# A long convolution beside a mixer MLP: the transform's split turned from 32 by 64 to 64 by 32 tokens, its second stages in eight-frequency fp32 units, the token matrices in fp16 parts

## The chip, the core and the metric

The kernel runs on one core of one Trainium2 chip. The metric is device time in microseconds (us). The core's engines run side by side, and each takes its own instructions strictly in order: TensorE (PE in the profile) multiplies matrices into PSUM, VectorE (DVE) and ScalarE (ACT) work elementwise, SyncE (SP) and, for some transfers, ScalarE issue DMAs. PEld is TensorE's weight loading.

## The reference

The reference normalises the input's rows, convolves them along the 2048 tokens with a kernel built from 128 complex states per channel (512 channels), and multiplies by the gate of an MLP on the same normalised rows:

```python
xn = layernorm(x)                                      # 2048 x 512
P  = exp(dt*A [:, :, None] * l)                        # 512 x 128 x 2048, complex
K  = einsum("dn,dnl,dn->dl", C, P, dt*B).real
y  = irfft(rfft(pad(xn.T)) * rfft(pad(K)))[:2048].T + xn*Dskip
h  = gelu(layernorm(xn) @ w1)
hs = concat(shift(h0,+1), shift(h1,-1), shift(h2,+2), shift(h3,-2)) @ w2
x1 = xn + hs
g  = silu(x1 + gelu(layernorm(x1) @ w3) @ w4)           # w3: 512 x 1376
out = x + y*g
```

Shifts are along the tokens, each of a quarter of the channels.

## The kernel before, in words

**Token layout.** 2048 tokens are 16 blocks of 128 partitions. Token number is a row r or t times a stride plus a column, and the kernel's transform of length 4096 uses the same split: 32 rows (`L1`) by 64 columns (`L2`). The transform is evaluated at 32 shifted frequencies g of the rows times 64 frequencies m of the columns, and the zero padding costs no work. It has a first stage (sums over rows, for each g) and a second stage (sums over columns, one small matrix per g, because the twiddle factors sit in it); the way back has the same two in reverse order.

**Stages of the transform.** `u_stage1` multiplies two token blocks of the normalised rows X by the matrix `ks1`; the result `ue` goes to a DRAM scratch, `scr_Ud`. `tables(hf)` builds the convolution kernel in chunks of 32 channels, 8 chunks for each half hf of the channels: exponentials and sines on ScalarE (`mag`, `wv`), products on VectorE, 64 matmul pairs per chunk (`pc<-wv`), an evacuation `kev`, and, at the end of `sums`, the first stage of the kernel's transform, named ks below: four matmuls `pc<-kev,ks`, two copies into `k1e`, two DMAs into scratch `scr_Kfa` or `scr_Kfb` (a and b are the halves). `products(hf)` is the second stage: it loads constants `cst`, the first-stage results of the rows, `uin`, and of the kernel, `kin`; multiplies both by the second-stage matrices (kspec and uspec); multiplies the two spectra on VectorE (`kh` is the evacuated kernel spectrum, `pr` the products); multiplies back (inv, `pd<-pr,cst`), copies to `z1e`, and stores to scratch `scr_Zda` or `scr_Zdb`. `inverse(hf,g)` loads `zin` from there, multiplies by `is2`, and multiplies the result into X, which by then holds the gate; `finish` adds the residual `xr` and stores the output.

In `products`, half 0 works in fp32 on two frequencies at a time, 16 units. Half 1 has 8 units of four frequencies, in two steps of two; there the loaded `kin` and `uin` are split in fp16 high and low parts (`kx`, `uh`) with power-of-two scales that `spectrum_scale` takes from the kernel's size, and kspec and uspec are three fp16 passes each.

**The MLP.** `token_mixing` makes X, the first stage of the rows, `h_pair` (rows times w1, gelu, kept as fp32 `hT`), the token shifts (`wrapped`), and `hs_pair` (four fp32 matmuls per token block with w2, added to X). Of the eight pairs of blocks four take fp32 w1 with transposes on TensorE and four take fp16 parts with DMA transposes. `mlp(g)`, eight times, is the wide MLP in fp16 high and low parts with w3 and w4, in three passes.

**What sets the order.** The functions above do not issue instructions. They record operations, and each operation's dependencies are found from the 32-partition quarters of SBUF places and PSUM banks that it touches. The table `ORDER` at the head lists the operations' numbers in the order of issue (a suffix a or v puts an evacuation or a scaling that either engine can do on ScalarE or VectorE). So one recorded list is cut up and interleaved by hand-held numbers; all recorded instructions carry one line of the profile, L330, that of the helper that issues them. PSUM is eight banks: pairs a and b for the MLP, pairs c and d for table sums, ks, spectra and the inverse stages. `Ring(place, bytes, n)` is a set of n buffers used in turn.

## Time and profile before

| | |
|---|---|
| three runs | 535.1, 536.88 (median), 538.08 us |
| profiled execution, span | 536.6 us, 13619 instructions |
| TensorE busy | 516.5 us |
| VectorE busy | 489.8 us |
| ScalarE busy | 425.2 us |
| last ks stage on TensorE starts | 398.92 us |
| last MLP matmul ends | 518.7 us |
| granted TensorE clock until 520 us, and after it | 1.00, 0.81 |

A span runs from the first to the last instruction of one profiled execution; here the span and the median of the runs agree within 0.3 us. Busy times are shares of the whole span, and the kernel has stretches of different kinds: loads and parameters (0 to 20 us); first half of the tables with token mixing (20 to 236); second half of the tables with the MLP and half 0 of the products (236 to 400); half 1 of the products with the rest of the MLP (400 to 520); and the end. In the rows of instruction groups a form like `pd<-kin,cst 128*64 128x256 f32` is destination, sources, the tile of TensorE's array (rows times columns), the shape and type of the operand. An fp32 matmul stands as two records in the trace, an fp16 one as one.

### The profile page before, as it was taken

The page shows a single profiled execution, that of the slowest core. Times are in us where ns is not written, and L with a number is a line of the kernel's source. Part 1 is how long each engine was busy: PE and PEld are TensorE (multiplying, and loading weights), DVE is VectorE, ACT ScalarE, POOL GpSimd, SP SyncE. Part 2 cuts the span into 40 slices and gives each one's busy share as a digit, 9 for nine tenths or more (in the row PEclk, how much of TensorE's full clock was granted, in tenths as well). Part 3 has the DMA queues.
Part 4 walks back from the last instruction along what each step waited for, and adds up shares of the span by engine and source line. Part 5 has one row for each costly group of instructions (what it writes and reads, how often), then busy time and mean ns, then how long its engine had stood idle before and what let it go on. Part 6 is the DMA issues. An engine that isn't in the chain of part 4 may idle for free.

```text
span 536.6 us, 13619 instructions
## 1 busy us (share of the span) xinstructions
PE 516.5 (96%) x5628; PEld 332.4 (62%) x5628; DVE 489.8 (91%) x755; ACT 425.2 (79%) x692; POOL 0.7 (0%) x6
## 2 busy tenths in 40 slices
PE   8999999999999999999999999999899899999992
PEld 7787664554475766565765666575565667666631
DVE  4999999999999999999999999999877799997277
ACT  3999999899899999999799897868646566774340
POOL 0000000000000000000000000000000000000000
PEclk9999999999999999999999999999999999999997
DMA  8989975689677325356375738838889969896997
GB/s 228 214 268 257 230 200 155 190 132 127 158 188 118 46 36 60 42 68 112 120 137 148 150 108 167 145 94 176 149 170 169 348 201 297 261 280 226 314 277 205
DMA packets 212830, 93.50 MB, mean 174 GB/s; under 512 B 163297, under 2 KB 196065, under 8 KB 212385
## 3 DMA queue, kind: packets, MB, share of 16 engines
q1 hardware_dynamic: 208032, 88.18, 71.3%
q10 hardware_dynamic: 4736, 4.46, 2.8%
q8 instruction: 44, 0.72, 0.6%
q14 instruction: 18, 0.14, 0.1%
HBM read 56.96 MB, written 29.36 MB: 161 GB/s over the span
## 4 chain that ended last, share of the span: by engine, by line
PE 63%; DVE 12%; ACT 11%; DMA 7%; issue 3%; SPq 1%; DVEq 0%; ACTq 0%
PE pb L330 24%; PE pa L330 17%; PE pd L330 11%; PE pc L330 11%; DVE wv L330 4%; DMA scr_Kfb<-k1e 3%; DVE X L330 3%; ACT wv L330 2%; ACT mag L330 2%; ACT L330 2%; SPq L330 1%; DMA kin<-scr_Kfb 1%; DMA scr_Kfa<-k1e 1%; DMA cst<-c_gq 1%; ACT g L330 1%
## 5 line engine op out<-in xcount | busy, mean ns | idle before, releaser
L330 PE MATMUL pb<-x1T,w3h 128*128 128x256 f16 (+1 forms) x1056 | 125.1, 273 | 1.2 <-ACT g L330 1.2
L330 PE MATMUL pa<-w4h,ghl 128*128 128x512 f16 (+1 forms) x528 | 123.2, 380 | 0.0
L330 PEld LDWEIGHTS <-w3h 128*128 128x128 f16 (+1 forms) x1056 | 102.3, 100 | 27.8 <-issue 11.0
L330 PEld LDWEIGHTS <-ghl 128*128 128x128 f16 (+1 forms) x528 | 49.3, 98 | 59.1 <-issue 8.7
L330 ACT ACT_TABLE_LOAD x52 | 66.7, 1283 | 2.0 <-PEq L1347 1.2
L330 ACT ACTIVATE wv<-wv 128x2080 f32<-128x2080 int32 x32 | 63.0, 1968 | 0.3 <-DVE wv L330 0.3
L330 ACT ACTIVATE g<-pb,wsc 128x512 f32<-128x512 f32 (+1 forms) x48 | 30.6, 651 | 12.8 <-PE pb L330 11.5
L330 ACT ACTIVATE ghl<-g,wsc 128x512 f16<-128x512 f32 (+1 forms) x39 | 26.6, 688 | 13.3 <-PE pa L330 8.3
L330 DVE TENSOR_TENSOR wv<-wv,eg 128x2048 f32<-128x2048 f32 x16 | 36.5, 2284 | 0.1
L330 DVE TENSOR_TENSOR wv<-mag,wv 128x2048 f32<-128x2048 f32 x16 | 36.6, 2285 | 0.0
L330 PE MATMUL pd<-pr,cst 64*128 64x256 f32 x256 | 36.3, 402 | 0.0
L330 PEld LDWEIGHTS pc<-wv 128*32 128x32 f32 x2048 | 29.8, 109 | 9.7 <-issue 6.2
L330 PE MATMUL pc<-wv 128*32 128x64 f32 x2048 | 32.5, 220 | 2.7 <-issue 1.9
L330 DVE SCALAR_TENSOR_TENSOR ghl<-g,wsc,ghl 128x512 f16<-128x512 f32 (+1 forms) x48 | 33.5, 701 | 1.0 <-ACT ghl L330 0.8
L330 ACT ACTIVATE wv<-wv,halfpi 128x2080 f32<-128x2080 f32 x16 | 32.9, 2056 | 0.1
L330 ACT ACTIVATE mag<-par 128x128 f32<-128x128 f32 x132 | 32.8, 441 | 0.0
L330 ACT ACTIVATE kh<-pc,ksc 128x256 f32<-128x256 f32 (+1 forms) x40 | 20.1, 553 | 14.1 <-PE pc L330 12.5
L330 PEld LDWEIGHTS pd<-pr,cst 64*128 64x128 f32 x256 | 22.0, 186 | 11.5 <-issue 8.3
L330 PE MATMUL pb<-xT,w 128*128 128x256 f32 x128 | 29.0, 382 | 0.0
L330 PEld LDWEIGHTS pb<-xT,w 128*128 128x128 f32 x128 | 23.8, 190 | 5.5 <-issue 1.6
L330 PE MATMUL pb<-w,hT 128*128 128x512 f32 x58 | 26.9, 599 | 0.0
L330 DVE BATCH_NORM_STATS2 stats<-X 128x6 f32<-128x512 f32 x32 | 21.4, 681 | 5.3 <-DMA X<-in_A_u_dram 5.3
(167 smaller groups left out, 882.7 us busy)
## 6 DMA issues: line engine op xcount, KB each, us to landing
wst<-in_B_w_dram SPq DMA_DIRECT2D x20, 512.0 KB, 4.0
scr_Ud<-ue SPq DMA_DIRECT2D x32, 256.0 KB, 3.2
scr_Kfa<-k1e SPq DMA_DIRECT2D x16, 256.0 KB, 6.2
uin<-scr_Ud SPq DMA_DIRECT2D x16, 256.0 KB, 4.1
cst<-c_gp SPq DMA_DIRECT2D x16, 256.0 KB, 3.5
kin<-scr_Kfa SPq DMA_DIRECT2D x16, 256.0 KB, 3.6
scr_Zda<-z1e SPq DMA_DIRECT2D x16, 256.0 KB, 3.0
scr_Kfb<-k1e SPq DMA_DIRECT2D x16, 256.0 KB, 6.0
```

The lines of the kernel that those rows point to most:

```text
L330: ins = [getattr(self.engines[op.eng], name)(*args, **kw).ins for name, args, kw in op.calls]
```

## The change

The split is turned: 64 rows (`NA`) by 32 columns (`NI`), with 64 frequencies g of the rows and 32 of the columns. With it:

- X is loaded and stored in two pieces of 64 partitions rather than four of 32, and the token shifts' wrap runs over 64.
- `u_stage1` has four matmuls with 64 rows and 128 columns of the array, rather than eight of 32 by 64.
- ks has eight matmuls of 32 by 128, 256 wide, into all four banks of c and d, rather than four 512 wide into c; four copies rather than two; one DMA in pieces of 128 bytes rather than two in pieces of 64.
- `products` has 8 units in each half, each of eight frequencies, all fp32: 16 matmuls each for kspec, uspec and inv on tiles of 64 by 32 or 32 by 64. The fp16 splits of half 1, their scales, the squares that fed them and `spectrum_scale` are gone. Loads and stores of half 0 double to 512 KB. In half 0 there is one buffer each for `kin` and `uin` (two before), and `z1e` lies in the place of `uin`.
- `inverse` has four matmuls of 128 rows and 64 columns, rather than eight of 64 by 32.
- The token matrices go to fp16 parts: seven of eight pairs in `h_pair` (four before), `hT` as high and low parts, w2 as `w2h` with a scale of its own (`second_weights`), twelve fp16 matmuls per block in `hs_pair` rather than four fp32 ones.
- Chunks 8 to 15 of the tables and units 0 to 7 of half 0 are recorded in turn, and `ORDER` is a new table.

The counts in the two orders: DMAs on SP 296 before and 230 now, on ScalarE's queue 36 and 19; VectorE instructions 757 and 776, ScalarE's 708 and 698.

```diff
@@ the order, the first line of each table
 ORDER = """
-23 20 21 0 22 39 7 8 1 6 5 105 86 3 2 106 107 108 109 110 111 112 87 89 88 90 113 91 114 115a 92 93 94 95 25 24
+4 78 3 31 5 6 0 7 79 80 81 8 88 89 82 83 90 91 92 84 85 22 86 93 94 2 95 87a 96a 21 97a 103 105 104 106 107 108 109
...
@@ tables: the kernel's first stage
-        if cc >= 8:
-            A.activation(kg.rearrange("p d i -> p i d"), kev, AF.Square, accum_out=ssk[:, cc - 8 : cc - 7])
-        pk = bank[2]
-            for r in range(4):
-                T.matmul(pk[n][64 * c : 64 * c + 64], ks1[rows], kev[rows]..., start=True, stop=True)
-        for n in range(2):
-            E.copy(k1e[:, :, n], pk[n].rearrange("p (i d) -> p i d", d=8))
-        for c in range(2):
-            Q.dma_start(K1d[cc // 8][:, :, :, ch : ch + 16]..., k1e[64 * c : 64 * c + 64]...)
+        pk = bank[2] + bank[3]
+            for hi in range(2):
+                for r in range(4):
+                    T.matmul(pk[r][:, :DH], kk1[rows, hi], kev[rows, NI * hi : NI * hi + NI]...,
+                        start=hi == 0, stop=hi == 1)
+        for r in range(4):
+            E.copy(k1e[:, :, 8 * r : 8 * r + 8], pk[r][:, :DH].rearrange("p (i d) -> p i d", d=8))
+        Q.dma_start(K1d[cc // 8][:, :, :, ch : ch + CQ].rearrange("i e g d -> (e g) i d"), k1e)
@@ buffers of the products: half 0, then half 1
-            kin=Ring(early, K2, 2), uin=Ring(early + 2 * K2, K2, 2), cst=Ring(early + 4 * K2, K2, 2),
-            kh=Ring(early + 6 * K2, K2, 1), pr=Ring(early + 7 * K2, K2, 2), z1e=Ring(early + 9 * K2, K2, 1),
+            kin=Ring(early, K4, 1), uin=Ring(early + K4, K4, 1), z1e=Ring(early + K4, K4, 1),
+            cst=Ring(early + 2 * K4, K2, 2), kh=Ring(early + 3 * K4, K2, 2), pr=Ring(early + 4 * K4, K2, 2),
-            pr=Ring(o, K4, 4), kh=Ring(o + 4 * K4, K4, 2), z1e=Ring(o + 6 * K4, K4, 3),
-            kx=Ring(o + 9 * K4, K4, 2), uh=Ring(o + 11 * K4, K4, 2),
+            pr=Ring(o, K2, 8), kh=Ring(o + 4 * K4, K2, 4), z1e=Ring(o + 6 * K4, K4, 3),
@@ products(hf, steps), one unit of eight frequencies
+            def spectrum(pair, src):
+                    for ri in range(2):
+                        for c in range(4):
+                            for h in range(2):
+                                T.matmul(both[h][32 * c : 32 * c + 32, ri], fwd[rows, c, 32 * ri : 32 * ri + 32],
+                                    src[rows, c], start=True, stop=True)
+            kp = spectrum(bank[3 - hf], kin)
+            kh = [ring["kh"]([P, 2, DH], F32, "kh") for _ in range(2)]
+            for h in range(2):
+                E.copy(kh[h], kp[h])
+            up = spectrum(bank[3], uin)
+            for h in range(2):
+                t = ring["pr"]([P, 2, DH], F32, "pr")
+                V.tensor_mul(t, up[h], kh[h])
+                V.tensor_mul(kh[h][:, ::-1], up[h], kh[h][:, ::-1])
+                V.tensor_sub(t[:, 0], t[:, 0], t[:, 1])
+                V.tensor_add(t[:, 1], kh[h][:, 0], kh[h][:, 1])
+            pz = [t[:, :DH] for t in bank[2] + bank[3]]
+                for ri in range(2):
+                    for c in range(4):
+                        for h in range(2):
+                            T.matmul(pz[c][64 * h : 64 * h + 64], inv[rows, h, ri], z[h][rows, ri],
+                                start=ri == 0, stop=ri == 1)
+            for c in range(4):
+                E.copy(z1e[:, c], pz[c])
+            Q.dma_start(by_g(Zd[hf], un), z1e.rearrange("p g d -> p (g d)"))
@@ inverse, u_stage1
-            for r in range(4):
-                for a in range(2):
-                    T.matmul(py[a][32 * r : 32 * r + 32], is2[h], zin[h, r], start=True, stop=True)
+            for a in range(2):
+                for r in range(2):
+                    T.matmul(py[a][64 * r : 64 * r + 64], is2, zin[:, 2 * a + r], start=True, stop=True)
-                for r in range(4):
-                    T.matmul(pu[r][64 * a : 64 * a + 64], ks1[rows], X[rows, s + a], start=True, stop=True)
+                for r in range(2):
+                    T.matmul(pu[2 * a + r], ks1[rows], X[rows, s + a], start=True, stop=True)
@@ h_pair, hs_pair
-            A.activation(hv, ph, AF.Gelu_apprx_tanh, scale=1.0 if j < HF else a1)
+            A.activation(h32, ph, AF.Gelu_apprx_tanh, scale=1.0 if j < HF else a1)
+            E.affine(hv[0], h32, sh)
+            V.scalar_tensor_tensor(hv[1], h32, sh, hv[0], op0=ALU.mult, op1=ALU.subtract)
-                    T.matmul(acc[i], w, w2s[m], start=m == 0, stop=m == 3)
+                    for n, (lh, lw) in enumerate(PASSES):
+                        T.matmul(acc[i], w[:, lh], w2h[m // 2][:, m % 2, lw],
+                            start=m == 0 and n == 0, stop=m == 3 and n == 2)
-            V.tensor_add(X[:, s], X[:, s], acc[i])
+            V.scalar_tensor_tensor(X[:, s], acc[i], a2, X[:, s], op0=ALU.mult, op1=ALU.add)
...
```

**SP around the last kernel writes.** SP issues nearly all DMAs, and an issue waits on SP until what it needs is there. `scr_Zda<-z1e` is the store of a unit of half 0, `uin<-scr_Ud` the load of a later unit's rows, `scr_Kfb<-k1e` the write of a chunk of the kernel's first stage. Before:

```order
L330 DMA uin<-scr_Ud 128x512
L330 DMA kin<-scr_Kfa 128x512
L330 DMA_TRANSPOSE x1T<-x1h 128x8x128
L330 DMA cst<-c_gp 128x512
L330 DMA scr_Kfb<-k1e 64x64x16
L330 DMA scr_Zda<-z1e 128x512
L330 DMA scr_Kfb<-k1e 64x64x16
L330 DMA uin<-scr_Ud 128x1024 x2
L330 DMA_TRANSPOSE x1T<-x1h 128x8x128
L330 DMA scr_Zda<-z1e 128x512
L330 DMA scr_Kfb<-k1e 64x64x16 x2
```

Now:

```order
L314 DMA scr_Zda<-z1e 2x64x1024
L314 DMA uin<-scr_Ud 128x1x1024
L314 DMA scr_Kfb<-k1e 128x32x32
L314 DMA cst<-c_gp 128x512
L314 DMA kin<-scr_Kfa 128x1x1024
L314 DMA scr_Zda<-z1e 2x64x1024
L314 DMA uin<-scr_Ud 128x1x1024
L314 DMA kin<-scr_Kfa 128x1x1024
L314 DMA scr_Kfb<-k1e 128x32x32
L314 DMA scr_Zda<-z1e 2x64x1024
L314 DMA uin<-scr_Ud 128x1x1024 x2
L314 DMA scr_Kfb<-k1e 128x32x32
```

A unit's store and the next unit's row load now stand next to each other, since they share a place, and the kernel writes of the last chunks stand behind such a pair.

**PE around the last ks stage.** The rows with `kev` are the ks stage of chunk 15, `pa<-w4h,ghl` is the MLP, `kin` and `uin` begin a unit of half 0. Before:

```order
L330 MATMUL pd_98<-pr,cst 128x256
L330 MATMUL pd_99<-pr,cst 128x256
L330 MATMUL pc_96<-kev,ks_80 64x512
L330 MATMUL pc_97<-kev,ks_80 64x512
L330 MATMUL pc_96<-kev,ks_80 64x512
L330 MATMUL pc_97<-kev,ks_80 64x512
L330 MATMUL pd_98<-kin,cst 64x256 x4
L330 MATMUL pd_99<-uin,cst 64x256 x4
L330 LDWEIGHTS ghl
L330 MATMUL pa_92<-w4h,ghl 128x512
```

Now:

```order
L314 MATMUL pd_97<-pr,cst 64x256 x2
L314 MATMUL pd_98<-pr,cst 64x256 x2
L314 MATMUL pc_95<-wv 32x64 x64
L314 MATMUL pc_95<-kev,kk_90 128x256
L314 MATMUL pc_96<-kev,kk_90 128x256
L314 MATMUL pd_97<-kev,kk_90 128x256
L314 MATMUL pd_98<-kev,kk_90 128x256
L314 MATMUL pc_95<-kev,kk_90 128x256
L314 MATMUL pc_96<-kev,kk_90 128x256
L314 MATMUL pd_97<-kev,kk_90 128x256
L314 MATMUL pd_98<-kev,kk_90 128x256
L314 LDWEIGHTS ghl
```

The ks stage takes all four banks; the inverse of a unit of half 0 stands ahead of the chunk's sums, and MLP matmuls now follow at once, with the last unit's spectra behind them.

**VectorE, one unit of half 1.** `kx` and `uh` are the fp16 parts, `pr` the products, `z1e` evacuations of the inverse. Before, most of one unit:

```order
L330 TENSOR_SCALAR kh<-pc_96,ksc 128x256
L330 TENSOR_TENSOR pr<-pc_97,kh 128x1024
L330 TENSOR_TENSOR pr<-pr 128x2x256
L330 COPY z1e<-pd_98 128x256
L330 TENSOR_SCALAR kx<-kin,ksc 128x1024
L330 SCALAR_TENSOR_TENSOR kx<-kin,ksc,kx 128x1024
L330 TENSOR_TENSOR pr<-pc_97,kh 128x1024
L330 SCALAR_TENSOR_TENSOR uh<-uin,uh 128x1024
L330 TENSOR_TENSOR pr<-pr 128x2x256
```

Now, a whole unit:

```order
L314 TENSOR_TENSOR pr<-pd_97,kh 128x512
L314 TENSOR_TENSOR pr<-pd_98,kh 128x512
L314 TENSOR_TENSOR kh<-pd_97,kh 128x2x256
L314 TENSOR_TENSOR kh<-pd_98,kh 128x2x256
L314 TENSOR_TENSOR pr<-pr 128x256
L314 TENSOR_TENSOR pr<-kh 128x256
L314 TENSOR_TENSOR pr<-pr 128x256
L314 TENSOR_TENSOR pr<-kh 128x256
L314 COPY z1e<-pc_96 128x256
```

The splits are gone, and all eight products and sums of a unit now stand in one row between its uspec and its inverse stage.

461 lines of the change are left out of this document (200 added, 261 removed), and 7 rows, old and new, of the table ORDER.

## The prediction

> **What bounds the kernel now.** I read the busy shares, then the stretches, then the chain of waits at the change from the tables to half 1, then single rows.
>
> ```profile
> PE 516.5 (96%) x5628; PEld 332.4 (62%) x5628; DVE 489.8 (91%) x755; ACT 425.2 (79%) x692; POOL 0.7 (0%) x6
> PE 63%; DVE 12%; ACT 11%; DMA 7%; issue 3%; SPq 1%; DVEq 0%; ACTq 0%
> ```
>
> By these two lines TensorE bounds it: 96% busy and 63% of the chain that ended last. The stretches say more (columns: stretch, length, busy time and count of PE, PEld, DVE, ACT, POOL, granted clock, DMA share, GB/s):
>
> ```profile
> 0.00:20.00 20.00, 17.09 (x117) 16.00 (x118) 12.25 (x46) 10.61 (x19) 0.70 (x6) 1.00 0.95 236
> 20.00:236.00 216.00, 213.59 (x2198) 134.76 (x2198) 212.02 (x335) 207.86 (x353) 0.00 (x0) 1.00 0.69 146
> 236.00:400.00 164.00, 160.91 (x2080) 102.96 (x2082) 159.06 (x203) 134.52 (x209) 0.00 (x0) 1.00 0.65 133
> 400.00:520.00 120.00, 118.38 (x1113) 76.52 (x1113) 94.32 (x149) 71.55 (x113) 0.00 (x0) 1.00 0.94 267
> 520.00:536.57 16.57, 6.56 (x128) 2.13 (x128) 12.10 (x25) 0.65 (x1) 0.00 (x0) 0.81 0.73 209
> ```
>
> Up to 400 us VectorE works 12.25 + 212.02 + 159.06 = 383.3 us and is idle for 16.7; TensorE is idle for 8.4. Both are full, so taking work from TensorE alone wins little there. Behind 400 TensorE is full and VectorE idle for 26 of 120 us. The last rows are an end of 16.6 us that VectorE fills. The boundary near 400 us is the last ks stage, and what follows it is a wait (start, us, what):
>
> ```profile
> 402.93 9.37 DMA scr_Kfb<-k1e
> 412.35 5.86 DMA kin<-scr_Kfb
> ```
>
> ```profile
> 398.92 1.09 PE L330 MATMUL pc<-kev,ks 32*64 32x512 f32 x8
> 487.23 1.13 PE L330 MATMUL pd<-pr,cst 64*128 64x256 f32 x8
> 518.68 0.66 PE L330 MATMUL pd<-zin,is 64*32 64x256 f32 x16
> ```
>
> So the span has four pieces: 400 to the last ks; 18.3 until kin of half 1 has landed (412.35 + 5.86); 70 of half-1 units until the last inverse stage ends (488.3); 48.3 behind it, of which 17.9 follow the last MLP matmul at 518.7. I forecast each piece. The profiled span is 536.6 us and the runs' median 536.9, so the sum needs no correction.
>
> **Ahead of the last ks: VectorE.**
>
> ```profile
> L330 DVE SCALAR_TENSOR_TENSOR ghl<-g,wsc,ghl 128x512 f16<-128x512 f32 x40 | 29.7, 745 | 0.9 <-ACT ghl L330 0.8
> L330 DVE COPY ue<-pa 128x512 f32<-128x512 f32 x6 | 4.0, 685 | 0.0
> ```
>
> Added: 16 splits of hT at the 0.745 us of the same form for ghl, 11.9; 14 splits of x2 at 0.745 in place of 8 subtractions of that width, at the 0.690 of the widest sum of pr in a later fence, +4.9; two splits of w2 at the 1.28 of the row of kx there and a chain of short operations for its scale, together about +4; 16 updates of X at 0.745 in place of additions from PSUM, at the 0.685 of the products there, +1. Gone: nine copies of ue, which the new order gives to ScalarE, -6.2; scalings and copies that the same order moves or drops, about -3.6. Sum +12: 395 us of VectorE work ahead of the last ks. ScalarE gains some 19 there (353 to 372) and TensorE loses 19 although 22 us of MLP have been moved ahead. With one engine clearly fullest its idle time should not grow beyond the 16.7 of now, nor vanish, since 7.8 of it lie in the first 20 us: 10 to 17. I take 15, last ks at **410**, 10 later than before.
>
> **TensorE** is relieved everywhere:
>
> ```profile
> 267.51 1.13 PE L330 MATMUL pd<-pr,cst 64*128 64x256 f32 x8
> 268.57 1.09 PE L330 MATMUL pc<-kev,ks 32*64 32x512 f32 x8
> 22.47 0.65 PE L330 MATMUL pa<-X,ks 32*64 32x512 f32 x2
> 23.52 1.99 PE L330 MATMUL pb<-xT,w 128*128 128x256 f32 x8
> 269.59 1.08 PE L330 MATMUL pd<-kin,cst 128*64 128x256 f32 x8
> 270.50 1.03 PE L330 MATMUL pd<-uin,cst 128*64 128x256 f32 x8
> 428.40 0.82 PE L330 MATMUL pc<-uh,cst 128*64 128x256 f16 x12
> 429.16 1.47 PE L330 MATMUL pa<-w4h,ghl 128*128 128x512 f16 x6
> 430.55 1.13 PE L330 MATMUL pd<-pr,cst 64*128 64x256 f32 x8
> 519.14 0.64 PE L330 MATMUL pc<-zin,is 64*32 64x256 f32 x16
> 85.37 10.46 PE L330 MATMUL pa<-w,hT 128*128 128x512 f32 x24
> L330 PE MATMUL pb<-x1T,w3h 128*128 128x256 f16 x960 | 113.7, 273 | 1.2 <-ACT g L330 1.2
> ```
>
> I go from start to start. Half 0 paid 0.91 twice and 1.06, 2.9 us in each of 16 steps, 46. A new stage is 16 small fp32 matmuls; the nearest row is the 64 by 32 tiles of zin, eight matmuls from 518.68 to 519.14, 0.46, so 0.92, and I take 0.95: 24 stages, 23 (-23). Half 1 paid 0.76 for each three-pass spectrum and 1.06 for the inverse, 2.58 in 16 steps, 41, and now pays 23 too (-18). w2: 64 fp32 matmuls at 10.46/12 = 0.87 were 56; 192 fp16 ones at 1.39/6 = 0.232 are 45 (-11). Three more pairs with fp16 w1, about -5. Against it, `u_stage1` pays two rounds of 0.87 rather than the 1.05 of 22.47 to 23.52, 8 times, +6; `inverse` two rounds of 0.46 for one, 16 times, +7; ks 8 matmuls, four side by side, two rounds of 0.46, nothing. Together about -45. None of it shortens the first piece, since VectorE is the fuller engine there; its worth shows only behind the last ks.
>
> **The wait for the kernel's spectrum.**
>
> ```profile
> scr_Kfb<-k1e SPq DMA_DIRECT2D x16, 256.0 KB, 6.0
> scr_Zdb<-z1e SPq DMA_DIRECT2D x8, 512.0 KB, 5.8
> uin<-scr_Ud SPq DMA_DIRECT2D x8, 512.0 KB, 5.7
> kin<-scr_Kfb SPq DMA_DIRECT2D x8, 512.0 KB, 6.0
> zin<-scr_Zdb SPq DMA_DIRECT2D x8, 512.0 KB, 7.0
> ```
>
> In the new order the last kernel write stands on SP behind the row load of half 0's last unit, which waits for the store of the unit before. That unit's inverse ends some 2 us ahead of the last ks (64 table matmuls stand between), so its 512 KB store, at the 5.8 us of half 1, lands about 4 behind it, and the write is issued there rather than after the 1 us that its four copies take. Write 6.0, load 6.0: 4 + 12 = **16**, against 18.3 now, where the write took 9.4. Pieces twice as long could make the write faster (3.0 us is what half 0's store of 256 KB in rows takes); a crowded stretch makes it 9.4. Bounds 13 to 20.
>
> **Eight units of half 1.** The constants row is a small load and hidden. Before, a step spread over the MLP; now each unit is in TensorE's order the same: kspec, uspec, 4.2 us of MLP (six w4 matmuls, 1.39, and two runs of twelve w3 matmuls at 113.7/960 = 0.118), inverse. VectorE stands between:
>
> ```profile
> L330 DVE TENSOR_TENSOR pr<-pd,kh 128x512 f32<-128x512 f32 x32 | 21.4, 685 | 0.6 <-ACT kh L330 0.2
> L330 DVE TENSOR_TENSOR pr<-pr 128x256 f32<-128x256 f32 x32 | 13.0, 422 | 0.4
> L330 DVE TENSOR_TENSOR pr<-pc,kh 128x1024 f32<-128x1024 f32 x16 | 19.5, 1222 | 1.7 <-ACT kh L330 1.3
> L330 DVE TENSOR_TENSOR pr<-pr 128x512 f32<-128x512 f32 x16 | 11.0, 690 | 0.4
> L330 DVE SCALAR_TENSOR_TENSOR kx<-kin,ksc,kx 128x1024 f16<-128x1024 f32 x8 | 10.3, 1282 | 0.2
> L330 DVE SCALAR_TENSOR_TENSOR uh<-uin,uh 128x1024 f16<-128x1024 f32 x8 | 9.7, 1216 | 0.0
> L330 ACT COPY z1e<-pd 128x256 f32<-128x256 f32 x47 | 16.2, 375 | 11.9 <-PE pd L330 10.2 <-DMA xr<-in_A_u_dram 1.5
> ```
>
> VectorE's half 1 falls from 19.5 + 11.0 + 10.3 + 9.7 = 50.5 us to 64 operations, 35.4. But four products at 0.685 and four sums at 0.422, 4.4 us, now stand in one chain between a unit's uspec and its inverse, with the 4.2 us of MLP beside them and hand-offs and a split of ghl among them: TensorE waits 0.4 to 1.1. The inverse writes all four banks of c and d, so the next kspec waits for two copies of bank c (0.375, one on each engine, with hand-offs 0.6). A unit is 3 x 0.95 + 4.2 + 0.6 + 0.4 to 1.1 = 8.0 to 8.8; I take 8.3, so **66**, against 70 now. All MLP without waits would be 7.05; without cover by the MLP a unit is 3 x 0.95 + 4.4 + 1.2 = 8.5.
>
> **The end.** Behind the last inverse the new order has 11.2 us of MLP (42 w4 matmuls at 0.232, 12 w3 at 0.118) and 28 zin matmuls, two at a time, 6.4: 17.6. Then follow, as now, products and residuals on VectorE and the last store, 17.9 in the trace; half of the zin work has the longer `inverse`, but VectorE sets the pace there (TensorE has 6.56 of 16.57 us). That is **35**, against 48.3. A second path agrees: the store of the last unit 1 + 5.8 and its reload 7.0 put the first reload at 14, and 13 reloads of 512 KB with three smaller loads, some 7 MB, take 26 at the 267 GB/s of the fourth stretch; the last inverse, product, sum and store add about 6, so 32. Range 31 to 40.
>
> Sum: 410 + 16 + 66 + 35 = **527**, which is +10, -2, -4 and -13 on the 536.6.
>
> The Trainium skill, "TensorE: Matmul & The Clock Gate", Part 3, "Measured speedup vs the span model", speaks against the small tiles: it gives four row tiles 3.07 times and sixteen tiles 10.6 times the rate of one matmul, which I read as an estimate of some 5.6 times for eight. By it a stage would take 16 x 0.46 / 5.6 = 1.3 us, and 24 stages behind the last ks 8 us more. The zin rows show eight tiles in the time of one, and go against it.
>
> **The rivals.**
>
> *The single place of uin and z1e in half 0 (slower).* A unit's row load waits until the unit before it has been stored, so one turn is uspec 0.95, chain 4.4 and hand-offs 1, inverse 0.95, copies 1, two issues 0.8, store, load: 9.1 plus 5.8 + 5.7 by half 1's rows of 512 KB, 20.6; by half 0's own rows,
>
> ```profile
> scr_Zda<-z1e SPq DMA_DIRECT2D x16, 256.0 KB, 3.0
> uin<-scr_Ud SPq DMA_DIRECT2D x16, 256.0 KB, 4.1
> ```
>
> 16.2, were size free. Half 0 runs at a DMA share of 0.65, not 0.94, so I place it near 17 to 18. By VectorE's work between successive uspecs in the new order, turns have 25.6, 17.1, 31.7, 19.1, 16.1, 15.2 and 11.7 us. At 17 the last three lag by 8, of which 5 fit in the idle time I allowed; at 20.6 the lag is 16 to 20, the last ks comes near 425, and the time is **542**. It decides from a turn of about 20.
>
> *The units serialise, and the end follows.* If hand-offs, ScalarE's copies of kh and the ghl splits make a unit 9.3 us, and SP's queue of half-1 loads and stores (0.94 DMA share now) holds the end at 37, it is 410 + 16 + 74.5 + 37 = **537**, no change. For it: nothing covers more than 4.2 us. Against it: VectorE has only about 7 us of work in a unit.
>
> *The tiles run less side by side.* From the trace, if they keep only the rate of the 32 by 64 tiles of `u_stage1` (8 x 0.87 in 1.05, 6.6 times), a stage takes 1.1 and the time is **531**; with 1.3, 535.
>
> *Better.* The order closes VectorE's idle time to 8, the write takes 4, units run at 7.5: 403 + 13 + 60 + 34 = **510**.
>
> **How the numbers follow.** Chances: likeliest 0.47 (own range 518 to 534), single place 0.17, serialised units 0.15, tiles 0.06, better 0.15. This kernel's measurement can tell 0.5%, 534.2 to 539.6, from no change. Faster: 0.45 + 0.15 + 0.04 and a little of the two middle rivals, 0.68; same 0.14, mostly from serialised units; slower 0.18. The range goes from the better case to the single place: 511 to 542.
>
> **What would show it.** Last ks at 407 to 414 with VectorE idle for 10 to 17 ahead of it. If it is later and the wait before uspec names the load of uin, the first rival is right. First half-1 kspec 13 to 20 behind it; stages of 0.9 to 1.0; units 8.0 to 8.8 apart; last MLP matmul 17 to 19 behind the last inverse. I am wrong in the main if VectorE ahead of the last ks falls short of 390 us or if units are over 9.

## The result

| | median of the runs, us | lowest to highest | ratio to before, 95% interval |
|---|---|---|---|
| before | 537.48 (4 runs) | 535.1 to 540.35 | |
| after | 915.66 (4 runs) | 913.75 to 918.92 | 1.703 [1.695, 1.710] |

The change makes the kernel 70% slower. The forecast was 527 with a range to 542, and none of the rivals reaches the measured time. Below, "after" is the changed kernel and "before" the one it came from.

The page of after, first the busy times, then the two lines of the chain that ended last:

```profile
PE 521.1 (57%) x6292; PEld 325.1 (36%) x6292; DVE 478.4 (52%) x774; ACT 414.8 (45%) x693; POOL 0.7 (0%) x6
DMA 46%; ACT 14%; DVE 13%; PE 11%; SPq 10%; issue 5%; ACTq 0%; DVEq 0%
DMA uin<-scr_Ud 14%; DMA scr_Zda<-z1e 10%; SPq L314 10%; DMA scr_Zdb<-z1e 6%; DVE wv L314 6%; ACT wv L314 3%; PE pd L314 3%; PE pa L314 3%; PE pb L314 3%; ACT mag L314 3%; DMA zin<-scr_Zda 2%; DMA scr_Kfb<-k1e 2%; DMA kin<-scr_Kfb 2%; PE pc L314 2%; DMA kin<-scr_Kfa 2%
```

Before, TensorE was 96% busy and 63% of the chain. Now no engine is busy for more than 57% of the span, and 46% of the chain are transfers, the units' loads and stores first. The stretches show where (stretch, length, busy time and count of PE, PEld, DVE, ACT, POOL, granted clock, DMA share, GB/s; cut at 250 us, at the last ks stage, at the first kspec of half 1, and at the end of the last inverse stage):

```profile
0.00:250.00 250.00, 224.12 (x2307) 149.66 (x2311) 231.24 (x397) 228.14 (x401) 0.70 (x6) 0.97 0.63 149
250.00:571.60 321.60, 177.58 (x2692) 111.70 (x2680) 163.43 (x211) 143.23 (x227) 0.00 (x0) 0.78 0.32 61
571.60:629.00 57.40, 12.29 (x136) 5.28 (x137) 10.25 (x22) 8.10 (x14) 0.00 (x0) 0.61 0.22 65
629.00:848.50 219.50, 74.90 (x990) 42.35 (x990) 48.28 (x98) 25.50 (x40) 0.00 (x0) 0.65 0.31 78
848.50:911.90 63.40, 32.21 (x182) 16.09 (x182) 25.17 (x48) 9.88 (x12) 0.00 (x0) 0.76 0.70 212
```

Up to 250 us VectorE is busy for 231 us, 92% of the time, and TensorE for 90%. From there to 848.5 us every engine is idle for much of the time, and the DMA queues are too: a share of 0.22 to 0.32 at 61 to 78 GB/s, where half 1 of before had 0.94 at 267 GB/s. So the transfers are late, and yet the engines that carry them are two thirds idle. The waits (engine, line, what for: us in all, times, longest):

```profile
PE pd L314 <- DMA uin<-scr_Ud: 159.5, 8, 39.2
DVE pr L314 <- PE pd L314: 204.8, 15, 40.5
```

Two turns of half 0 in the chain (start, us, what):

```profile
316.23 12.84 DMA scr_Zda<-z1e
329.09 13.08 DMA uin<-scr_Ud
355.87 13.43 DMA scr_Zda<-z1e
369.32 12.78 DMA uin<-scr_Ud
```

A turn takes 355.87 - 316.23 = 39.6 us, of which store and load are 25.9; the first rival had 20.6 for it, with 5.8 + 5.7 for the two transfers. Within the store from 356 to 369 us:

```profile
356.00:369.00 13.00, 7.66 (x97) 5.60 (x96) 9.16 (x12) 10.91 (x31) 0.00 (x0) 0.89 0.12 42
```

A share of 0.12 of 16 DMA engines is about two engines. The packet records of the trace say the same. Counted from them: how many packets of 4096 bytes there were in a stretch, how long one took, and how many were under way at once, most often (while any was) and at most:

```
kernel   stretch, us      packets   median ns   at once: most often   at most
after    356 to 369           128         159                      2         4
before   412.3 to 413.6        95         159                     16        19
```

A packet takes the same 159 ns as before, but two are under way most of the time (77% of it) and not sixteen. 512 KB are 128 packets, 64 for each of two engines: 64 x 0.159 = 10.2 us; the chain has 12.8 to 13.4 from issue to landing.

What the transfers have in common is their form in the order. In half 1 of before, `scr_Zdb` and `uin` were `128x1024`, and kin of the same shape. In the changed kernel the scratch side of a unit is `r s e (h g) d -> h (r s e) (g d)` with h = 2: 64 rows of 4 KB for each half of the frequencies, and the order prints the store as `2x64x1024`. The outermost count of that side is 2. This holds for uin, kin and z1e of all 16 units, 48 transfers.

### The profile page after: what moved, and what is told of

Read it like the earlier page. It is cut to its first block, busy times and chain, and to the rows that moved or that the text cites. A ratio compares the mean times of both kernels' runs of the same rounds, so it can differ in the third digit from the quotient of the medians.

```text
span 911.9 us, 14810 instructions
## 1 busy us (share of the span) xinstructions
PE 521.1 (57%) x6292; PEld 325.1 (36%) x6292; DVE 478.4 (52%) x774; ACT 414.8 (45%) x693; POOL 0.7 (0%) x6
## 4 chain that ended last, share of the span: by engine, by line
DMA 46%; ACT 14%; DVE 13%; PE 11%; SPq 10%; issue 5%; ACTq 0%; DVEq 0%
DMA uin<-scr_Ud 14%; DMA scr_Zda<-z1e 10%; SPq L314 10%; DMA scr_Zdb<-z1e 6%; DVE wv L314 6%; ACT wv L314 3%; PE pd L314 3%; PE pa L314 3%; PE pb L314 3%; ACT mag L314 3%; DMA zin<-scr_Zda 2%; DMA scr_Kfb<-k1e 2%; DMA kin<-scr_Kfb 2%; PE pc L314 2%; DMA kin<-scr_Kfa 2%
## 5 line engine op out<-in xcount | busy, mean ns | idle before, releaser
L314 PE MATMUL pb<-x1T,w3h 128*128 128x256 f16 (+1 forms) x1056 | 136.7, 290 | 23.1 <-DMA x1T<-x1h 19.2
L314 PEld LDWEIGHTS <-w3h 128*128 128x128 f16 (+1 forms) x1056 | 108.7, 106 | 56.8 <-issue 24.0
L314 DVE TENSOR_TENSOR pr<-pd,kh 128x512 f32<-128x512 f32 x32 | 20.8, 686 | 204.8 <-PE pd L314 204.8
L314 PE MATMUL pd<-uin,cst 64*32 64x256 f32 x512 | 29.4, 591 | 159.5 <-DMA uin<-scr_Ud 159.5
L314 PEld LDWEIGHTS pd<-uin,cst 64*32 64x32 f32 x512 | 13.3, 154 | 170.7 <-issue 169.7
L314 PE MATMUL pc<-kin,cst 64*32 64x256 f32 x256 | 14.5, 583 | 103.6 <-DMA cst<-c_gp 63.7
L314 ACT COPY z1e<-pc 128x256 f32<-128x256 f32 x22 | 8.2, 377 | 143.4 <-PE pd L314 129.9
L314 PE MATMUL pb<-xT,w1h 128*128 128x256 f16 x336 | 39.4, 276 | 3.0 <-DVE stats L314 2.7
L314 PE MATMUL pd<-kin,cst 64*32 64x256 f32 x256 | 11.6, 475 | 48.9 <-issue 30.8
L314 PEld LDWEIGHTS <-w1h 128*128 128x128 f16 x336 | 32.7, 99 | 13.0 <-DVE stats L314 3.5
```

Source lines behind the costliest of these rows:

```text
L314: ins = [getattr(self.engines[op.eng], name)(*args, **kw).ins for name, args, kw in op.calls]
```

## Experiments

The theory: **a transfer whose pattern has 2 as its outermost count is carried by two of the 16 DMA engines**; all the lost time follows from these 48 transfers. Its rivals: the single place of uin and z1e in half 0, which was rival one of the prediction and stands in the chain, and the new stages or the new order themselves.

**Two DMAs of 64 partitions each.** Bytes, places and order stay; each of the 48 transfers is issued as two, of one half of the partitions each. Not shown below: whoever waited for the one transfer now waits for both.

```diff
-                Q.dma_start(t.rearrange("p g d -> p (g d)"), by_g(dr, un))
+                with plan.together():
+                    for h in range(2):
+                        Q.dma_start(t[64 * h : 64 * h + 64].rearrange("p g d -> p (g d)"), by_g(dr, un)[h])
...
-            Q.dma_start(by_g(Zd[hf], un), z1e.rearrange("p g d -> p (g d)"))
+            with plan.together():
+                for h in range(2):
+                    Q.dma_start(by_g(Zd[hf], un)[h], z1e[64 * h : 64 * h + 64].rearrange("p g d -> p (g d)"))
```

> The changed kernel, but each 512 KB transfer of uin, kin and z1e is issued as two of 64 partitions, one for each half of the frequencies. Same addresses, same pieces of 4 KB, same order, same shared place. Theory A (a transfer whose scratch side is a pattern with an outermost count of 2 is worked by 2 of the 16 DMA engines): the pieces now spread over all engines, a transfer falls from about 13 us to 3 to 6, the turn of half 0 from 40 to about 20 us, the granted clock returns to about 1, and the time is 520 to 545 us. Rival B (the addresses or the size of the pieces are slow): transfers stay at about 13 us and the time at 880 to 930. Rival C (the order or the shared place of uin and z1e is the cause, whatever the transfers take): above 800.

Measured: 565.94 us (563.08 to 567.59), ratio 1.051 [1.044, 1.057] to before. 350 of the 378 us are gone with an edit that changes neither a byte nor an instruction of the computing engines. The expectation's 520 to 545 was missed all the same: 28 us over before remain, so not all of the lost time follows from the 48 transfers being on two engines. Its stretches, cut at the last ks, the first kspec of half 1 and the last inverse, are the four pieces of the prediction:

```profile
0.00:425.90 425.90, 392.00 (x4988) 259.14 (x4988) 394.50 (x607) 371.21 (x627) 0.70 (x6) 0.98 0.61 134
425.90:441.20 15.30, 11.56 (x136) 4.96 (x137) 9.36 (x20) 7.78 (x14) 0.00 (x0) 0.89 1.03 221
441.20:519.40 78.20, 64.27 (x990) 41.23 (x990) 48.98 (x100) 25.68 (x42) 0.00 (x0) 0.91 0.86 220
519.40:564.30 44.90, 28.77 (x182) 14.10 (x182) 24.88 (x48) 9.93 (x13) 0.00 (x0) 0.90 1.02 300
```

**Before, with its rows turned.** The opposite edit: the kernel before keeps its stages and its order, and only half 1's 24 transfers get the outermost count 2. The rows of a unit then land on other partitions, and the constants are permuted to match, so that the same is computed.

```diff
+            two = lambda rows: rows.rearrange("(x h) f -> h x f", h=2)
-            Q.dma_start(uin, Ud[hf][:, :, :, g0 : g0 + 2 * nb].rearrange("r s e g d -> (r s e) g d"))
+            Q.dma_start(uin.rearrange("p g d -> p (g d)"), two(u_rows) if hf else u_rows)
...
-            Q.dma_start(kin, K1d[hf][:, :, g0 : g0 + 2 * nb].rearrange("i e g d -> (i e) g d"))
+            Q.dma_start(kin.rearrange("p g d -> p (g d)"), two(k_rows) if hf else k_rows)
...
+            Q.dma_start(two(z_rows) if hf else z_rows, z1e.rearrange("p b a d -> p (b a d)"))
```

> The kernel before, with only the 24 loads and stores of 512 KB in half 1 changed: partition 64h + x takes row 2x + h of the scratch, so that the scratch side has an outermost count of 2 that cannot be merged; the constants of half 1 are permuted alike, and what is computed is the same. The set of addresses and the pieces of 4 KB are those of before, two rows apart. Theory A: each transfer needs 64 pieces on each of two engines, 64 x 0.159 = 10.2 us of them, alone about 12 to 13 us; 24 transfers are 245 us in a row, so half 1 takes 250 rather than 70 us and the time is 660 to 730 us. Rival B (piece size or address set): 530 to 545, as before. Rival C (the new order or shared place): 530 to 545.

Measured, in one run: 726.82 us. Its last ks stage and its last inverse:

```profile
398.78 1.09 PE L332 MATMUL pc<-kev,ks 32*64 32x512 f32 x8
655.65 1.13 PE L332 MATMUL pd<-pr,cst 64*128 64x256 f32 x8
```

The last ks stands where it stood before (398.92), and from there to the end of the last inverse it is 258.0 us, against 89.4. 24 transfers at 10.2 us, one behind the other on the same two engines, are 245; two packets are under way for 79% of the piece. So the pattern costs this in the kernel before as well, without any of the new stages.

**Other counts.** The same edit with an outermost count of 4, and of 16:

```diff
-            two = lambda rows: rows.rearrange("(x h) f -> h x f", h=2)
+            two = lambda rows: rows.rearrange("(x h) f -> h x f", h=4)      # and h=16
```

> The kernel before with the 24 transfers of half 1 turned as in the earlier run, but with an outermost count of 4 rather than 2. Theory A: four engines, 32 x 0.159 = 5.1 us of packets in each, 24 transfers 122 us in a row; half 1 takes 115 to 150 us from the last ks to the last inverse stage, against 88 before and 257 with a count of 2; time 565 to 610 us. Rival (any row order that cannot be merged is slow): 700 or more. Rival (only a count of 2 is special): 533 to 545.

> The same with an outermost count of 16. Theory A: all 16 engines, time 533 to 545, as before. Rival (any row order that cannot be merged is slow): 600 or more.

| outermost count in half 1's transfers of before | time, us | last ks to the end of the last inverse, us | in this piece, packets of 4096 bytes: median ns | while any is under way, most often at once |
|---|---|---|---|---|
| 128 rows (before) | 537 to 538 | 89.4 | 159 | 16 |
| 16 | 548.4 | 99.3 | 211 | 16 |
| 4 | 618.93 | 164.1 | 159 | 4 |
| 2 | 726.82 | 258.0 | 159 | 2 |

The edited kernels ran once each, and those with 4 and 16 came out 9 and 3 us above their ranges. With 4 a transfer has 32 packets to an engine, 5.1 us, and 24 of them 122; the piece is 42 us longer than that, so packets are not all of it. The time falls with the count as the theory says, and the number of packets under way is the count itself; 16 nearly brings the time back, which refutes the rival that any such order of rows is slow. That 16 still costs 10 us goes with packets of 211 ns; no run takes this apart.

The Trainium skill, "DMA: Bandwidth & Descriptors", "Why a DMA increments its semaphore by 16 and not by 1", states the rule: a DMA is spread over the largest number of engines, 16 at most, that divides the slowest dimension above 1 of both its patterns. By it the counts 2, 4 and 16 give 2, 4 and 16 engines, and these runs agree: 2, 4 and 16 packets under way most often.

**A place of its own for z1e.** Half 0's z1e lies in the place of kh instead of uin's; once with the slow transfers, once with the split ones.

```diff
-            kin=Ring(early, K4, 1), uin=Ring(early + K4, K4, 1), z1e=Ring(early + K4, K4, 1),
+            kin=Ring(early, K4, 1), uin=Ring(early + K4, K4, 1), z1e=Ring(early + 3 * K4, K4, 1),
```

> The changed kernel, but z1e of half 0 lies in the place of kh, not of uin, so that a row load need not wait for the store before it. Transfers stay as they are. Rival C (the shared place is the cause): each of eight turns loses the 13 us of the store, 100 us or more, time below 815. Theory A: a unit still keeps the two engines busy for 3 x 10.2 = 31 of the 40 us of a turn, so at most 9 us go from each turn in half 0 and nothing in half 1: 840 to 915 us, transfers still 12 us and more.

> Both edits: transfers in two halves, and z1e of half 0 in the place of kh. Theory A with the turn no longer binding: within 1% of the run with halves alone. If the shared place costs what the prediction's first rival says (a turn of 20 us), it is 10 to 16 us below that run. Rivals B and C as there: B near 880 to 930, C below 815.

Measured: 902.96 us in one run with the slow transfers, 13 below after; 554.36 (549.6 to 557.84) with the split ones, 11.6 below the run with the shared place, ratio 1.027 [1.019, 1.035] to before. Both are in their expected ranges. The shared place is a real cost of the size that rival one gave it (15), and no more: it explains 12 of 378 us. The pieces of the second:

```profile
0.00:418.10 418.10, 387.04 (x4985) 257.74 (x4985) 394.24 (x607) 371.37 (x627) 0.70 (x6) 0.98 0.62 136
418.10:432.60 14.50, 10.29 (x136) 4.72 (x136) 10.14 (x22) 7.99 (x14) 0.00 (x0) 1.00 1.06 231
432.60:510.90 78.30, 63.84 (x990) 39.64 (x990) 48.19 (x98) 25.39 (x40) 0.00 (x0) 0.93 0.87 220
510.90:556.00 45.10, 28.56 (x189) 14.01 (x182) 24.89 (x48) 9.83 (x12) 0.00 (x0) 0.93 1.01 299
```

Some of its units in half 1 (start, us, what, and in brackets how long TensorE waited and for what):

```profile
444.68 1.22 PE L314 MATMUL pc<-kin,cst 64*32 64x256 f32 x32 [2.33 <-issue]
452.27 1.21 PE L314 MATMUL pc<-kin,cst 64*32 64x256 f32 x32 [0.43 <-ACT z1e L314]
460.28 4.46 PE L314 MATMUL pb<-x1T,w3h 128*128 128x256 f16 x24 [3.60 <-DMA x1T<-x1h]
467.36 1.22 PE L314 MATMUL pc<-kin,cst 64*32 64x256 f32 x32 [1.57 <-DVE ghl L314]
476.29 1.22 PE L314 MATMUL pc<-kin,cst 64*32 64x256 f32 x32 [1.79 <-DMA cst<-c_gp]
483.93 1.20 PE L314 MATMUL pc<-kin,cst 64*32 64x256 f32 x32 [0.49 <-DVE z1e L314]
486.74 0.59 PE L314 MATMUL pd<-uin,cst 64*32 64x256 f32 x2 [1.62 <-DMA uin<-scr_Ud]
496.14 1.20 PE L314 MATMUL pc<-kin,cst 64*32 64x256 f32 x32 [0.51 <-DVE z1e L314]
```

From 444.68 to 452.27 and from 476.29 to 483.93 a unit takes 7.6 us; the one that begins at 483.93 waits for uin and takes 12.2, and the longest, from 452.27, waits for a transposing load of the MLP (x1T) and takes 15.1. In the stretch of the units the packets of 4096 bytes are slow: 242 ns (median) with up to 20 at once, against 159 before.

**Whole rows.** If that is so, rows of a unit that lie in one piece in the scratch need neither the count of 2 nor the halves. The scratch tensors keep the frequencies' upper half as their first dimension; the second stage's transfers become 128 rows of 4 KB. The price is paid elsewhere: the first stage's writes, of rows and kernel, and the reloads of zin go in two DMAs each, those of the kernel and of zin to every second partition.

```diff
-    Ud = dram.tile([2, 2, S, 2, NG, DH], F32, name="scr_Ud")
+    Ud = dram.tile([2, 2, 2, S, 2, NG // 2, DH], F32, name="scr_Ud")
...
-        return dr.rearrange("r s e (h g) d -> h (r s e) (g d)", h=2)[:, :, 4 * DH * un : 4 * DH * (un + 1)]
+        return dr.rearrange("h r s e g d -> (h r s e) (g d)")[:, 4 * DH * un : 4 * DH * (un + 1)]
...
-        Q.dma_start(zin, Zd[hf][2 * g : 2 * g + 2].rearrange("s r e g d -> (e g) (s r) d"))
+        with plan.together():
+            for h in range(2):
+                Q.dma_start(zin[h::2], Zd[hf][h, 2 * g : 2 * g + 2].rearrange("s r e g d -> (e g) (s r) d"))
```

> The changed kernel with z1e of half 0 in the place of kh, and the scratch laid out by halves of the 64 frequencies, with the first stage's columns in the order (real or imaginary, frequency within the half, half). A transfer of the second stages is then 128 rows at one stride, one DMA to all 128 partitions; in exchange the first stage's writes and the last stage's loads go in two DMAs each, to every second partition. In the run with two halves of 64 partitions the 4 KB packets of half 1 took 0.25 us, against 0.159 before. Theory D (64 neighbouring partitions take only part of the rate; late loads are what makes a unit of half 1 take 9.9 rather than the 8.3 us forecast): packets return to 0.16 us, units to 9 us or less, time 535 to 548 us. Rival E (the loads are late because of where SP's order puts them): 550 to 558, as with halves.

Measured: 562.57 us (558.42 to 563.52), ratio 1.043 [1.036, 1.050]. The first piece, the units and the end:

```profile
0.00:424.90 424.90, 389.49 (x4988) 258.91 (x4988) 394.27 (x607) 371.44 (x627) 0.70 (x6) 0.97 0.58 135
437.80:509.70 71.90, 59.90 (x990) 38.22 (x990) 48.24 (x99) 25.41 (x40) 0.00 (x0) 0.95 0.83 239
509.70:560.70 51.00, 32.86 (x182) 16.36 (x182) 25.42 (x48) 9.94 (x12) 0.00 (x0) 0.81 0.88 263
```

The packets are back at 159 ns and the units are 6.4 us shorter than in the split kernel with a place of its own. But the first piece is 6.8 longer, in which SP issues 64 writes `scr_Ud<-ue` and not 32, and the end 5.9, at a granted clock of 0.81 where that kernel had 0.93. The expectation of 535 to 548 was missed; what the rows win is lost in the two pieces with the two-part writes and reloads. That these are the cause is argued; no run puts them back one by one.

**The loads earlier.** On top of the whole rows, SP's loads and stores are moved forward in `ORDER` as far as their places allow, with five places for uin and kin in half 1 rather than three.

```diff
-            uin=Ring(late, K4, 3), cst=Ring(late + 3 * K4, K2, 4), kin=Ring(late + 5 * K4, K4, 3),
+            uin=Places(late, late + K4, late + 2 * K4, o + 9 * K4, o + 10 * K4), cst=Ring(late + 3 * K4, K2, 4),
+            kin=Places(late + 5 * K4, late + 6 * K4, late + 7 * K4, o + 11 * K4, o + 12 * K4),
```

> The same, and: SP's loads, kernel writes and stores from unit 1 of half 0 on are issued as soon as the order has passed what they depend on (the table lists unit 5's row load behind those of units 6 and 7), with five places each for uin and kin of half 1 and three for xr. Nothing else moves. Rival E: units of half 1 fall to 8 us, the wait ahead of them by 1 to 2, time 515 to 535. Theory D alone: within 1% of the run without this edit.

Measured: 564.98 us (563.13 to 568.05), ratio 1.050 [1.044, 1.056]. This is within 1% of the run without the edit, as expected if the rate of 64 partitions had been the whole cause of the long units, but the pieces say otherwise. The first units of half 1:

```profile
447.93 1.96 PE L318 MATMUL pc<-kin,cst 64*32 64x256 f32 x32 [11.03 <-DMA kin<-scr_Kfb]
456.84 1.21 PE L318 MATMUL pc<-kin,cst 64*32 64x256 f32 x32 [0.43 <-ACT z1e L318]
464.42 1.21 PE L318 MATMUL pc<-kin,cst 64*32 64x256 f32 x32 [0.43 <-ACT z1e L318]
472.09 1.10 PE L318 MATMUL pc<-kin,cst 64*32 64x256 f32 x32 [0.51 <-DVE z1e L318]
```

With their loads in time, units start 7.5 to 7.7 us apart, all but the first, and all eight take 61.4 us, under the forecast's 66. But the loads that were moved forward stand ahead of kin on SP, which came 11 us late. So the run gained in one piece and lost in the one before, and its end was some 52 us.

**The loads in time, kin first.** From the split kernel with a place of its own: kin alone in whole rows, the first kin loads right behind the last kernel write on SP, five places, residual rows earlier.

```diff
-    K1d = [dram.tile([NI, 2, NG, DH], F32, name=f"scr_Kf{h}") for h in "ab"]
+    K1d = [dram.tile([2, NI, 2, NG // 2, DH], F32, name=f"scr_Kf{h}") for h in "ab"]
...
+            Q.dma_start(kin.rearrange("p g d -> p (g d)"), Kd[:, 4 * DH * un : 4 * DH * (un + 1)])
```

> The run with two halves and z1e in the place of kh, and three more edits: kernel writes to every second partition so that kin is one transfer of 128 rows (rows' loads and stores stay two halves, the first and last stages as in the changed kernel); SP's loads and stores issued as soon as the order allows, but the first two kin right behind the last kernel write; five places for uin and kin of half 1, three for xr, whose later loads are issued earlier. The run with whole rows and SP's order had units of 7.5 us but kin 11 us late. If late loads are all that separates half 1 from its forecast: last ks 418 (as with two halves), wait 14 to 17, eight units 60 to 64 us, end 40 to 45 us, time 532 to 545. If the rate of 64-partition transfers still binds, units of 9 us and 548 to 556.

Measured: 552.25 us (551.99 to 554.8), ratio 1.027 [1.022, 1.032], no better than without the edit, and above the range of 532 to 545. Six of the eight units take 7.1 to 7.7 us and the first 9.2; one does not:

```profile
460.55 5.28 PE L317 MATMUL pb<-x1T,w3h 128*128 128x256 f16 x24 [8.62 <-DMA x1T<-x1h]
```

The unit from 448.5 takes 19 us: the transposing load of the MLP is late, and on SP it is issued behind uin, cst and kin of later units and a store. Without the edit TensorE waited 3.6 us for it, now 8.6: the lateness was passed on to this load. Its eight units take 73.1 us, 9.1 on the average, and so fit the expectation's other case in size (units of 9 by the rate of 64 partitions), but not in cause.

**Fewer bytes at the end.** Much of what is left over the forecast is the end, 45 against 35. In two kernels, the split one with a place of its own and the one with its loads in time, half 1's residual rows are cut to a quarter: one row of four is loaded, and it is added to all four, so three quarters of these loads are left out and the result is another.

```diff
-            by_r(xr, xv[:, :, 4 * k : 4 * k + 4, ch], load=(Q, A))
+            by_r(xr, xv[:, :, 4 * k : 4 * k + rows, ch], load=(Q, A))       # rows = 1 in half 1
...
+        rows = xr.to_broadcast([P, s1 - s0, DH]) if hf else xr[:, s0 % 4 : s0 % 4 + s1 - s0]
```

> Leaves out three of every four rows of the residual that half 1 reloads at its end (64 KB a load, not 256 KB; the first row of four is added to all four), on top of the kernel with the transfers in two DMAs and the place of its own. About 1.7 MB less crosses the DMA queues behind the last units, and at the some 300 GB/s of that kernel's end that is 5.8 us. Theory: the end is 45 and not 35 because the forecast counted the reloads of zin and left out what shares the queues with them. Then the end falls to 37 to 40 and the time to 546 to 549. Rival: the end is set by VectorE and the stages, as the forecast had it for the first of its two paths, and the loads are hidden: end 43 to 45, time 552 to 556.

> The same edit on the kernel whose loads of half 1 are issued as early as their places allow. Besides the end (45.4 there) it has one unit of 19 us in which TensorE waits 8.6 us for a transposing load behind a full queue; some of the residual rows are loaded in that stretch. Theory that the bytes in the queues explain what is left: the end falls to 38 to 41, the long unit by 2 to 6, time 539 to 545. Rival, that the bytes do not matter and the order on the queue does: end as before, 550 to 554.

Measured: 555.21 us (552.15 to 555.86), ratio 1.028 [1.022, 1.035], and 553.82 (552.54 to 554.32), ratio 1.026 [1.019, 1.033]: nothing gained in either. The end of the first, then that of the kernel with its loads in time and that of the second run:

```profile
509.00:554.10 45.10, 28.74 (x182) 14.20 (x182) 24.87 (x48) 9.83 (x12) 0.00 (x0) 0.90 0.98 285
```

```profile
504.80:550.20 45.40, 28.76 (x188) 13.91 (x182) 24.81 (x48) 9.94 (x12) 0.00 (x0) 0.90 0.88 266
507.30:552.50 45.20, 28.78 (x182) 13.90 (x182) 24.80 (x48) 9.94 (x12) 0.00 (x0) 0.90 0.89 268
```

45.1 and 45.2 us, as without the edit. But length times GB/s gives the bytes that moved in the end: 13.5 MB in the split kernel with a place of its own and 12.9 in the first run, 12.1 MB in the kernel with its loads in time and 12.1 in the second run. The edit took 0.6 MB out of the end, about 2 us at 285 GB/s, and nothing in the second, where these rows had been loaded earlier; so neither run tests the theory as the 1.7 MB expected would have. What speaks against it is another pair: the kernel with its loads in time has 1.4 MB less in its end than the one without, and the end is as long.

**Reloads ahead of output stores.** From the kernel with its loads in time, SP's reloads of zin stand in the order as soon as their places are free, ahead of the output stores, which wait for VectorE. The operations are given here by name, in `ORDER` by number (zin0.3 is the fourth reload of half 0, finish0.5 a store of the output).

```diff
-... finish0.5 (out), zin1.5, finish0.1 (out), zin1.6, finish0.3 (out) ...
+... zin0.3, zin0.4, zin0.5, zin1.1, zin1.0, zin1.2, zin0.6, zin1.4, zin1.7, zin1.3, zin1.5, zin0.7, zin1.6, then the stores
```

> The kernel whose loads of half 1 are issued as early as their places allow, with one edit more: behind the store of the last unit, SP's reloads of both halves' results (zin) stand in its order as soon as their places are free, ahead of the output stores, which wait for VectorE. The end was 45.4 us there. Theory that the order on SP holds the end (a reload stands behind a store that waits for VectorE): 13 reloads and the residuals, some 9 MB, at about 300 GB/s are done some 30 us behind the last unit's store, and the end falls to 37 to 41; time 544 to 548. Rival, that the end is bound by the sum of all bytes there, the output's 4 MB too, whatever their order: end 44 to 47, time 551 to 555.

Measured: 554.42 us (553.99 to 556.82), ratio 1.030 [1.022, 1.037]. Its end, and then TensorE's waits for reloads in it:

```profile
505.30:552.20 46.90, 28.54 (x182) 13.86 (x182) 24.87 (x48) 9.94 (x12) 0.00 (x0) 0.90 0.89 258
```

```profile
PE pd L317 <- DMA zin<-scr_Zda: 3.7, 1, 3.7
PE pc L317 <- DMA zin<-scr_Zda: 2.9, 2, 1.7
```

46.9 us, no shorter; the theory on the order falls. The number is in the rival's range, but the rival (the sum of all bytes) doesn't go well with 12.1 and 13.5 MB in ends of the same length. What makes the end 45 us long stays open. No version that beats the kernel before was found.

## Why the prediction was wrong

The pieces, in us:

| piece | before | forecast | after | two DMAs | two DMAs, place of its own |
|---|---|---|---|---|---|
| to the last ks | 400.0 | 410 | 571.6 | 425.9 | 418.1 |
| wait for the kernel's spectrum | 18.3 | 16 | 57.4 | 15.3 | 14.5 |
| units of half 1 | 70 | 66 | 219.5 | 78.2 | 78.3 |
| end | 48.3 | 35 | 63.4 | 44.9 | 45.1 |
| span | 536.6 | 527 | 911.9 | 564.3 | 556.0 |

The first two columns are cut as in the prediction, at the end of the last ks stage and where kin has landed; the others where the last ks stage (about 1 us earlier) and the first kspec of half 1 start.

**The step that failed** is the price of a unit's transfers: "its 512 KB store, at the 5.8 us of half 1", "Write 6.0, load 6.0", and in rival one "9.1 plus 5.8 + 5.7 by half 1's rows of 512 KB". It took size for price: in the changed kernel such a transfer took 12.8 to 13.4 us. The rows were those of other patterns: the order showed `2x64x1024` and `128x1x1024` where before had `128x1024`, both stood in the part on the change, and the prediction didn't ask what the pattern does. The bounds were drawn from transfers that all had 64 or 128 rows as their outermost count, so they could not hold it. The rule of the Trainium skill quoted above speaks against this change, more than the packing rule that the prediction weighed: with two engines and the 159 ns of a packet, half 1's 24 transfers come to 245 us where the forecast had 16 + 66 = 82, and a turn of half 0 to 9.1 + 20.4 = 29.5. By half 1 alone that is 527 + 163 = 690, slower beyond doubt.

**Wrong in kind: the bottleneck.** All four pieces were summed on TensorE and VectorE, with transfers hidden but for named waits. In the changed kernel a unit's transfer is in the way from 250 us on. "I am wrong in the main if VectorE ahead of the last ks falls short of 390 us or if units are over 9": units are 27 us, though VectorE's work was as forecast.

**VectorE ahead of the last ks**: forecast 395 us, measured 394.2 to 394.5. Right. Its idle time was to be 10 to 17, and not to grow beyond the 16.7 of before; without the slow transfers and with a place of its own it is 418.1 - 394.2 = 23.9, and the last ks is 8 late. Three waits of the first piece of that run, for the input, for a transposing load and for ScalarE:

```profile
DVE stats L314 <- DMA X<-in_A_u_dram: 7.8, 5, 3.2
DVE x2h L314 <- DMA xT<-x2h: 2.2, 1, 2.2
DVE hT L314 <- ACT h L314: 2.2, 1, 2.2
```

Before, up to 400 us, has the first and neither of the others:

```profile
DVE stats L330 <- DMA X<-in_A_u_dram: 5.3, 1, 5.3
```

That is 6.9 us of the 7.2 by which the idle time grew. No run tested these.

**The stages** were right: 0.95 forecast, 0.86 to 0.9 from kspec to uspec where nothing waits (444.68 to 445.54 in the split kernel with a place of its own). The rival in which the tiles run less side by side, and the 1.3 us worked out from the Trainium skill with it, is refuted. TensorE's busy time fell from 516.5 to 489.7 us there, by 27 and not by the 45 of the forecast's terms; ahead of the last ks it fell from 391.6 to 387.0, by 4.6 where 19 were forecast. The rows do not say which term was short, and it did not decide, since VectorE is the fuller engine there.

**The wait for the kernel's spectrum**, 16: 15.3 and 14.5 once the transfers are repaired. Right in size, with its terms right only then.

**Units**, 8.3 each in 8.0 to 8.8: 7.5 to 7.7 with loads in time, below the range: TensorE waits 0.43 to 0.51 us ahead of a kspec, where 0.6 was added, and the rows have no wait ahead of the inverse, where 0.4 to 1.1 was added. But they take 9.8 on the average in the split kernels, since loads are late: those of the units, x1T, and once, for 1.79 us, the constants, which the prediction took as hidden. The second rival had the size (9.3 and no change in all) and the wrong cause: it had said that VectorE's chain and ScalarE's copies would do it.

**The end**, 35: 45. The forecast's two paths agreed, 35 and 32, and both were short by 10 or more, so that they agreed was luck. The second path is 26 + 6 and leaves out the 14 us that it gives to the first reload; and it counted "some 7 MB" of loads, where 299 GB/s for 45.1 us are 13.5 MB, the output's stores among them. At the path's own 267 GB/s these would be 50 us. That term was mis-sized, but bytes alone do not set the length either, as 12.1 MB took as long. SP's order does not explain it.

**Rival one**, the single place: priced at 15, measured at 11.6 to 13. With the transfers split, the last full turns from uspec to uspec are 18.6 and 19.6 us with the shared place, and 17.6 and 15.7 without, near the 20 from which it was to decide; its own two transfers were mis-priced by the failed step.

The split kernel with a place of its own has a profiled span of 556.0, 29 above the forecast: +8 in the first piece, -1.5 in the wait, +12 in the units (late loads) and +10 at the end. Only the units' part was taken away by a run (61.4 us with loads in time); no run took all of them away at once.

## What to carry to other kernels

A transfer is priced by its pattern, not by its size: before a row of the old kernel is used for a new transfer, compare the order of their dimensions, the outermost count first, on both sides. When transfers are late while the DMA share is low, look at how many packets are under way at once; 0.12 of 16 engines is two engines. Whole rows for one stage moved the strided side to other transfers here, and those have to be priced too.

## What the runs showed of the hardware that was not expected

- **Few engines.** With an outermost count of 2, 4096-byte packets took 159 ns as ever, most often two at once; 512 KB took 12.8 to 13.4 us where 128 rows took 5.7 to 6.0.
- **Slow packets.** From the last ks to the last inverse, 4096-byte packets took 242 and 256 ns (medians) in the two split kernels, where a unit's transfers have 64 partitions, and 211 with 16 as the outermost count of 128, with 20 to 22 at once at most, against 159 for 128 rows. The Trainium skill, "SBUF — State Buffer", "Door 1: The DMA port swizzle", has 64 partitions reach half of the memory's ports and gives 196 against 328 GB/s, a factor of 1.67; here a packet takes 242/159 = 1.52 and 256/159 = 1.61 times as long, which is near it. That the count of 16 has slow packets too was measured and is not explained.
- **The clock.** Where TensorE waited, its granted clock fell to 0.61 and 0.65 (stretches of after), and a matmul of uspec took 591 ns on the average, against 402 in the split kernel with a place of its own:

```profile
L314 PE MATMUL pd<-uin,cst 64*32 64x256 f32 x512 | 29.4, 591 | 159.5 <-DMA uin<-scr_Ud 159.5
```

```profile
L314 PE MATMUL pd<-uin,cst 64*32 64x256 f32 x512 | 21.9, 402 | 4.9 <-DMA uin<-scr_Ud 4.5 <-ACT kh L314 0.4
```
